# Two interleaved attention and MLP layers on one core: five of ten stretches of the instruction order rearranged

## The chip, the cores and the metric

The kernel runs on one core of a Trainium2 chip. The metric is the device time of one execution in microseconds (us). Before the change the median of three runs is 442.16 us (441.85 to 442.31).

The engines in the text are PE (TensorE, matrix products), DVE (VectorE), ACT (ScalarE), POOL (GpSimd) and SP (SyncE, which issues the DMAs). PEld is PE's weight load, which runs beside its products. Each engine works through a queue of its own in order; semaphores make one engine wait for another.

## The reference

An attention layer A and an MLP layer B act on x of 2048 rows and 512 columns, and the pair is applied twice, with the same weights, in bf16. Cut to what matters:

```python
qkv = (x @ wqkv) ...                     # 32 heads of 16 columns
scores = einsum("bhqd,bhkd->bhqk", q, k) * Dh ** -0.5
mask = (i - j >= 0) & (i - j < 256)      # sliding window of 256 rows
p = softmax(where(mask, scores, -1e9))
A = einsum("bhqk,bhkd->bhqd", p, v) ... @ wo

B = gelu(x @ w1 + b1) @ w2 + b2          # w1: 512 x 1792, w2: 1792 x 512

x = x + A(layernorm(x)); x = x + B(layernorm(x))   # and both lines once more
```

## The kernel before

**Tiles and stages.** The 2048 rows are 16 tiles of 128 rows; with two passes there are 32 tiles. Attention works on blocks of 256 rows, 16 in all, numbered on through both passes (block b of the text is the b-th). The MLP works on ten jobs of two or four tiles (`JOBS`).

For one block of attention the steps are, with the lines of the program: layer norm (`bn_stats` and `bn_aggr` on DVE, L599 and L601; two small steps on POOL for the reciprocal root, L611 and L617; `xn` on DVE, L627), a transposing DMA on SP (L632) into `xnTA`, projections to q, k and v on PE (L653) with evacuations from PSUM (q and v: a cast on DVE L588 or ACT L590; k: L687 on DVE, which multiplies by a parity mask and writes `KT`), scores on PE (L754, a "score group" of four PSUM banks), Exp on ACT (L761, two for each group, into `E`), a multiplication of parts of `E` by `mask01` (L782, on DVE or on POOL), the P·V products on PE (L804; two for each block), a transpose of their result on DVE (L813, `OD`), reciprocal and normalisation (L817, L821), a second transpose (L827), the output projection on PE (L653 again, from `OT` and `Wo_sb`) and the residual addition on DVE (L849). For a job of the MLP: layer norm and transposing DMA into `xnTB`, products with `W1_sb` on PE (L653), for six of the 14 row chunks a bias addition on DVE (L871) and Gelu on ACT (L874), for the others Gelu with bias on ACT (L879), products with `W2_sb` (L653), and the residual addition (L887 on POOL, L894 on DVE). The bf16 values of a V tile are copied once more, shifted by half a tile, with DMAs (L702).

**What sets the order.** The whole program is first recorded as a list of 3098 nodes, each an operation with what it reads and writes (`_Plan.add`). It is then issued in the order of a table of node numbers, `_ORDER`. A second table, `_ALT`, names the nodes that run on their alternative engine (masks and normalisations: POOL for DVE; casts: ACT for DVE). A third, `_BANKS`, gives the PSUM bank for each allocation in the order in which the allocations come. The program is thus interleaved by hand-made tables, not by a planner at build time:

```python
for i in _ALT:
    nodes[i]["eng"], nodes[i]["fn"] = nodes[i]["alts"][1]
banks = iter(_BANKS)
...
for i in _ORDER:
    nd = nodes[i]
    assert nd["deps"] <= seen
    ...
    for g, k in nd["alloc"]:
        b = next(banks)
        gmap[g] = tuple(range(b, b + k))
```

`_Sched.op` then goes through the nodes in this order and puts each into the queue of its engine, with semaphore waits for what it reads, for the buffers that it overwrites and for the earlier users of its PSUM banks. So a bank number can make one instruction wait for another that has nothing to do with its data. Attention of a block, projections for the next two blocks and pieces of MLP jobs stand mixed on PE's queue, and the same on the others.

## Time and profile before

| | before |
|---|---|
| median of the runs (lowest, highest) | 442.16 us (441.85, 442.31) |
| span of the profiled execution | 442.4 us |
| PE busy | 416.1 us (94%) |
| ACT busy | 386.4 us (87%) |
| DVE busy | 341.0 us (77%) |
| POOL busy | 212.7 us (48%) |
| instructions | 16864 |

The profile is one execution; its span is the time from its first to its last instruction, and it stands 0.24 us above the median of the runs. A row of a timeline gives the start, the length, the engine, the line, the operation, the tiles that it writes and reads and, in brackets, the idle time ahead of it with what ended that. A row of the groups gives, after the count, busy time and the mean length of one in ns, then the idle time ahead of the group. The first slices of the span are the load of x and the weights; the last are the second pass's MLP alone.

### The profile page before, as it was taken

Reading aid. Unit: us, or ns where it says so; the run is one execution under the profiler, and the core shown is the slowest. Engines: PE = TensorE matmul, PEld = TensorE weight load, DVE = VectorE, ACT = ScalarE, POOL = GpSimd, SP = SyncE. Lnnn points to the kernel's source line nnn. Section 1 sums busy time; section 2 is a strip of 40 time slices with the busy share of each in tenths; the row PEclk is TensorE's granted clock in tenths of the full one; section 3 lists DMA queues with packets and bytes.
Section 4 is the critical chain, followed back from the end, with each engine's and each line's share of the span. In section 5 each row is a group of like instructions: output and inputs, shape, how many; then the busy total and the mean of one; then the engine's idle time right before and its main releaser. Section 6 shows DMA issues by size and latency. Waiting matters only on the chain.

```text
span 442.4 us, 16864 instructions
## 1 busy us (share of the span) xinstructions
PE 416.1 (94%) x7523; PEld 233.2 (53%) x7593; DVE 341.0 (77%) x638; ACT 386.4 (87%) x458; POOL 212.7 (48%) x236
## 2 busy tenths in 40 slices
PE   8997999988789997999999999999999999999997
PEld 4555657544444563554455455455555464444675
DVE  7997789788785599967698868877888576746762
ACT  4997999999889999889899989999897988999533
POOL 3566344363442674711575454634728165804411
PEclk9999999999899999999999999999999999999999
DMA  7686422004101012121031021100421014003002
GB/s 234 184 209 185 87 64 45 20 10 69 39 3 25 16 34 56 28 46 24 4 65 31 1 57 26 34 20 10 69 39 20 20 39 105 14 1 81 15 0 73
DMA packets 48116, 23.25 MB, mean 53 GB/s; under 512 B 33196, under 2 KB 48044, under 8 KB 48044
## 3 DMA queue, kind: packets, MB, share of 16 engines
q1 hardware_dynamic: 48044, 22.17, 22.2%
q8 instruction: 60, 0.98, 0.9%
q14 instruction: 12, 0.10, 0.1%
HBM read 8.00 MB, written 2.10 MB: 23 GB/s over the span
## 4 chain that ended last, share of the span: by engine, by line
PE 79%; ACT 11%; DVE 6%; issue 2%; DMA 1%; DVEq 0%
PE ps L653 59%; PE ps L754 9%; PE ps L804 9%; ACT E L761 9%; DVE OD L813 1%; PE ps L539 1%; DVE stat L599 1%; DVE X L849 1%; DMA xnTB<-xn 1%; ACT gT L879 1%; ACT L879 1%; DVE KT L687 1%; DVE E L782 0%; PE ps L639 0%; ACT QT L590 0%
## 5 line engine op out<-in xcount | busy, mean ns | idle before, releaser
L761 ACT ACTIVATE E<-ps 128x1024 bf16<-128x1024 f32 x300 | 284.2, 1033 | 28.7 <-PE ps L754 28.0
L782 POOL TENSOR_TENSOR E<-E,mask 128x512 bf16<-128x512 bf16 (+2 forms) x111 | 120.9, 1106 | 91.3 <-ACT E L761 91.0
L653 PE MATMUL ps<-W_sb,gT 128*128 128x512 bf16 (+1 forms) x434 | 112.2, 373 | 3.2 <-issue 2.2
L653 PE MATMUL ps<-xnTB,W_sb 128*128 128x512 bf16 (+1 forms) x541 | 107.8, 336 | 3.4 <-issue 1.8
L653 PEld LDWEIGHTS ps<-xnTB,W_sb 128*128 128x128 bf16 x560 | 52.0, 98 | 42.9 <-issue 4.1
L653 PE MATMUL ps<-xnTA,Wqkv_sb 128*128 128x256 bf16 x512 | 70.7, 273 | 0.9 <-ACT E L761 0.4
L782 DVE TENSOR_TENSOR E<-E,mask 128x512 bf16<-128x512 bf16 (+2 forms) x125 | 60.1, 500 | 13.3 <-ACT E L761 12.9
L754 PE MATMUL ps<-QT,KT 32*128 32x128 bf16 (+3 forms) x1920 | 60.3, 231 | 9.8 <-ACT E L761 5.6
L653 PEld LDWEIGHTS ps<-W_sb,gT 128*128 128x128 bf16 x462 | 41.2, 98 | 41.1 <-issue 3.6
L754 PEld LDWEIGHTS ps<-QT,KT 32*128 32x128 bf16 x1920 | 28.5, 92 | 59.1 <-ACT E L761 34.9
L653 PEld LDWEIGHTS ps<-xnTA,Wqkv_sb 128*128 128x128 bf16 x512 | 47.4, 98 | 20.2 <-issue 2.9
L813 DVE STREAM_TRANSPOSE OD<-ps 128x1024 f32<-128x1024 f32 x32 | 39.9, 1246 | 21.3 <-PE ps L804 20.7
L887 POOL TENSOR_TENSOR Xb<-X,b2all 128x512 f32<-128x512 bf16 x32 | 37.7, 1180 | 34.3 <-DVE X L894 33.9
L879 ACT ACTIVATE gT<-ps,b1T 128x512 bf16<-128x512 f32 (+1 forms) x80 | 42.6, 609 | 9.5 <-PE ps L653 9.4
L804 PE MATMUL ps<-E,Va 64*17 64x128 bf16 (+3 forms) x1920 | 44.3, 234 | 1.9 <-issue 0.8
L821 POOL TENSOR_TENSOR Nb<-OD,Rc 128x512 bf16<-128x512 f32 x25 | 26.4, 1058 | 38.7 <-DVE Rc L817 29.8
L804 PE MATMUL ps<-E,Vs 64*17 64x128 bf16 (+3 forms) x1920 | 44.9, 234 | 0.0
L599 DVE BATCH_NORM_STATS2 stat<-X 128x6 f32<-128x512 bf16 x64 | 42.9, 679 | 0.5
L804 PEld LDWEIGHTS ps<-E,Va 64*17 64x17 bf16 x1920 | 37.2, 85 | 11.6 <-issue 9.0
L871 DVE TENSOR_SCALAR gT<-ps,b1T 128x512 bf16<-128x512 f32 (+1 forms) x60 | 36.8, 632 | 6.6 <-PE ps L653 6.2
L687 DVE TENSOR_TENSOR KT<-ps,parmask 128x1024 bf16<-128x1024 f32 x32 | 38.7, 1211 | 3.6 <-PE ps L653 3.6
L804 PEld LDWEIGHTS ps<-E,Vs 64*17 64x17 bf16 x1920 | 38.0, 85 | 0.2
(55 smaller groups left out, 348.8 us busy)
## 6 DMA issues: line engine op xcount, KB each, us to landing
Vs<-Va SPq DMA_DIRECT2D x64, 68.0 KB, 2.0
W_sb<-in_B_w_dram SPq DMA_DIRECT2D x4, 512.0 KB, 4.8
out_dram<-X SPq DMA_DIRECT2D x15, 128.0 KB, 1.8
X<-in_A_x_dram SPq DMA_DIRECT2D x3, 512.0 KB
Wqkv_sb<-in_A_wqkv_dram SPq DMA_DIRECT2D x4, 256.0 KB, 4.5
W_sb<-in_B_w_dram SPq DMA_DIRECT2D x2, 384.0 KB, 7.1
W_sb<-in_B_w_dram SPq DMA_DIRECT2D x1, 768.0 KB, 5.0
Wqkv_sb<-in_A_wqkv_dram SPq DMA_DIRECT2D x1, 512.0 KB, 6.7
```

The costliest lines, as they stand in the source:

```text
L599: add("dve", lambda e, B, t=t, k6=k6: e.bn_stats(stat6[:, k6, :], X[:, t, :]), reads=["X%d" % t], writes=["st%d" % k6], key="bs%d" % (k + j))
L653: r = e.matmul(ps[:, B[g][0], cols], lhsT, rhs, start=st, stop=sp)
L687: add("dve", lambda e, B, g=g, i=i: e.tensor_tensor(out=KT[:, kb, 2 * i : 2 * i + 2].rearrange("p c m a q -> p a (c m) q"), in0=ps[:, B[g] ...
L754: x = e.matmul(ps[:, bk[r], o : o + n], KT[rows, kb, c, m].rearrange("p a q -> p (a q)"), QT[rows, c, q : q + n], start=True, stop=True)
L761: add("act", lambda e, B, g_=g_, gi=gi: e.activation(E[:, 2 * gi : 2 * gi + 2, e0 : e0 + 512], ps[:, B[g_][0] : B[g_][0] + 2, :], AF.Exp, ...
L782: fn = lambda e, B: e.tensor_tensor(out=Ew, in0=Ew, in1=Mw, op=ALU.mult)
L804: x = e.matmul(ps[32 * r : 32 * r + VW, B[g][par], c % 2 * 2 * P + lo : c % 2 * 2 * P + hi], V[rows, (2 * b + m // 2) % VR, c * HC + 2 * r ...
L813: add("dve", lambda e, B: e.transpose(OD[:, s].rearrange("p a c q -> p (a c q)"), ps[:, B[g][0] : B[g][0] + 2, :]), reads=["ps:" + g], wri ...
L821: return e.tensor_tensor(out=Nb[:, s, :].rearrange("p (k a d) -> p a k d", a=2, d=Dh), in0=sums[:, :, :, 0:Dh], in1=rc[:, :, :, None].to_b ...
L871: add("dve", lambda e, B, g=g, fc=fc: e.tensor_scalar(out=gT[:, fc, c0 : c0 + M], in0=ps[:, B[g][0], 0:M], scalar1=b1T[:, fc : fc + 1], sc ...
L879: add("act", lambda e, B, g=g, fc=fc: e.activation(gT[:, fc, c0 : c0 + M], ps[:, B[g][0], 0:M], AF.Gelu_apprx_tanh, bias=b1T[:, fc : fc + ...
L887: add("pool", lambda e, B, t=t, xs=xs: e.tensor_tensor(out=Xb[:, xs, :], in0=X[:, t, :], in1=b2all[:], op=ALU.add), reads=["X%d" % t, "b2a ...
```

## The change

The three tables get other numbers. The program's order has nine places that no operation crosses, and with them ten stretches. In five of these the nodes stand in another order; in the other five the queue of each engine is as it was. The stretches that change lie, by the times of the profile before, at 0 to 31.2 us, 31.2 to 67.5, 110.7 to 160.7, 160.7 to 198.0 and 290.2 to 341.4; they are called the first, second, fourth, fifth and eighth in the text. `_ALT` has 162 entries in place of 172: DVE has 16 operations more, POOL 15 less and ACT one less. The 15 from POOL are ten masks (L782), two normalisations (L821) and three of the small layer-norm additions (L611); casts change between DVE and ACT in both directions, one net to DVE. 139 of 658 bank numbers differ. Nothing else of the program changes; its lines after the tables stand 7 lower in number (L842 is what L849 was).

```diff
 _ORDER = [
-    15, 34, 5, 0, 6, 14, 35, 7, 33, 28, 38, 29, 47, 8, 18, 23, 9, 36, 3, 26, 31, 10, 57, 37, 11, 22, 1, 40, 4, 24,
...
+    34, 0, 15, 5, 8, 35, 3, 14, 6, 16, 38, 23, 47, 33, 19, 4, 29, 9, 36, 7, 57, 1, 21, 10, 37, 11, 28, 58, 40, 12, 61,
...
 _ALT = [
...
 _BANKS = [
```

The first place is DVE's queue in the second stretch, where block 3 is projected and block 1 is attended to; before the change it runs at 33 to 40 us. `KT` is the evacuation of a K projection, `E` a mask, `xn` the layer norm's result, `OD` the transpose behind a P·V product. Before:

```order
L782 TENSOR_TENSOR E<-E,mask01 128x4x128
L782 TENSOR_TENSOR E<-E,mask01 128x4x192
L849 TENSOR_TENSOR X<-X,ps 128x512 x2
L599 BN_STATS stat6<-X 128x6 x2
L601 BN_AGGR statmv<-stat6 128x2 x2
L687 TENSOR_TENSOR KT<-ps,parmask 128x2x8x64
L627 TENSOR_SCALAR xn<-X,statmv,rstd 128x512 x2
L813 STREAM_TRANSPOSE OD<-ps 128x1024
L687 TENSOR_TENSOR KT<-ps,parmask 128x2x8x64
```

And now:

```order
L775 TENSOR_TENSOR E<-E,mask01 128x4x128
L842 TENSOR_TENSOR X<-X,ps 128x512
L775 TENSOR_TENSOR E<-E,mask01 128x4x64
L592 BN_STATS stat6<-X 128x6
L775 TENSOR_TENSOR E<-E,mask01 128x4x192 x2
L842 TENSOR_TENSOR X<-X,ps 128x512
L680 TENSOR_TENSOR KT<-ps,parmask 128x2x8x64
L592 BN_STATS stat6<-X 128x6
L594 BN_AGGR statmv<-stat6 128x2 x2
L806 STREAM_TRANSPOSE OD<-ps 128x1024
L620 TENSOR_SCALAR xn<-X,statmv,rstd 128x512 x3
L680 TENSOR_TENSOR KT<-ps,parmask 128x2x8x64
```

A mask of 64 columns for each of four parts (256 in all) and one of 192 (768) have come in ahead of the second `KT`, the two `xn` of this block's MLP input stand behind the `OD` transpose, and a third `xn` stands with them.

The second place is PE's queue at the same time, from the end of block 1's first P·V product. Scores have `QT,KT`, projections `xnTA`, the MLP `xnTB`. Before:

```order
L653 MATMUL ps<-xnTA,Wqkv_sb 128x256 x12
L754 MATMUL ps<-QT,KT 128x256 x8
L653 MATMUL ps<-xnTA,Wqkv_sb 128x256 x6
L754 MATMUL ps<-QT,KT 128x192 x8
L754 MATMUL ps<-QT,KT 128x128 x4
L653 MATMUL ps<-Wqkv_sb,xnTA 128x512 x8
L754 MATMUL ps<-QT,KT 128x192 x8
L754 MATMUL ps<-QT,KT 128x128 x4
L653 MATMUL ps<-xnTB,W1_sb 128x256 x8
```

And now:

```order
L747 MATMUL ps<-QT,KT 128x256 x8
L646 MATMUL ps<-xnTA,Wqkv_sb 128x256 x12
L747 MATMUL ps<-QT,KT 128x192 x8
L747 MATMUL ps<-QT,KT 128x128 x4
L646 MATMUL ps<-xnTA,Wqkv_sb 128x256 x4
L646 MATMUL ps<-Wqkv_sb,xnTA 128x512
L747 MATMUL ps<-QT,KT 128x192 x8
L747 MATMUL ps<-QT,KT 128x128 x4
L646 MATMUL ps<-Wqkv_sb,xnTA 128x512 x7
L747 MATMUL ps<-QT,KT 128x128 x8
L747 MATMUL ps<-QT,KT 128x64 x16
L646 MATMUL ps<-xnTB,W1_sb 128x256 x16
```

The first score group has moved ahead of twelve projection products, the second ahead of a few, and the last score group (128x128 and 128x64) ahead of the MLP's first pieces. The first V projection (`Wqkv_sb,xnTA`) now stands ahead of a score group, and its bank is the one that the second `KT` evacuation frees.

The third place is DVE's queue in the fourth stretch, behind block 4's first P·V product, with the bias additions (`gT`) of the third MLP job; before the change it runs at 119 to 126 us. Before:

```order
L813 STREAM_TRANSPOSE OD<-ps 128x1024
L871 TENSOR_SCALAR gT<-ps,b1T 128x512
L599 BN_STATS stat6<-X 128x6
L871 TENSOR_SCALAR gT<-ps,b1T 128x512
L782 TENSOR_TENSOR E<-E,mask01 128x4x128
L817 RECIPROCAL Rc<-OD 128x32
L871 TENSOR_SCALAR gT<-ps,b1T 128x512 x2
L782 TENSOR_TENSOR E<-E,mask01 128x4x192
L871 TENSOR_SCALAR gT<-ps,b1T 128x512
L782 TENSOR_TENSOR E<-E,mask01 128x4x192
```

And now:

```order
L806 STREAM_TRANSPOSE OD<-ps 128x1024
L810 RECIPROCAL Rc<-OD 128x32
L775 TENSOR_TENSOR E<-E,mask01 128x4x128
L864 TENSOR_SCALAR gT<-ps,b1T 128x512
L775 TENSOR_TENSOR E<-E,mask01 128x4x128
L864 TENSOR_SCALAR gT<-ps,b1T 128x512
L775 TENSOR_TENSOR E<-E,mask01 128x4x128
L775 TENSOR_TENSOR E<-E,mask01 128x4x64
L864 TENSOR_SCALAR gT<-ps,b1T 128x512
L775 TENSOR_TENSOR E<-E,mask01 128x4x64
L864 TENSOR_SCALAR gT<-ps,b1T 128x512
L775 TENSOR_TENSOR E<-E,mask01 128x4x192
```

More masks stand between the bias additions; they come from POOL's queue and from earlier or later places on DVE's.

## The prediction

> **What bounds the kernel now.** I read the page's busy line first, then the windows of each reordered stretch, and last the timelines of all engines in the places where TensorE (PE) stands still.

> ```profile
> PE 416.1 (94%) x7523; PEld 233.2 (53%) x7593; DVE 341.0 (77%) x638; ACT 386.4 (87%) x458; POOL 212.7 (48%) x236
> ```

> PE is the bound on average. The windows below are cut at the ends of the stretches (the third is left as it is); after the start, their columns are length, then busy time of PE, PEld, DVE, ACT and POOL, PE's granted clock, DMA share and GB/s.

> ```profile
> 0.00:31.20 31.20, 28.14 (x409) 17.21 (x413) 28.06 (x57) 25.22 (x33) 15.77 (x31) 1.00 0.78 205
> 31.20:67.50 36.30, 33.52 (x576) 21.02 (x579) 30.07 (x62) 32.85 (x43) 17.75 (x19) 1.00 0.47 119
> 67.50:110.70 43.20, 39.36 (x908) 24.29 (x905) 36.33 (x68) 41.32 (x52) 21.02 (x22) 1.00 0.20 35
> 110.70:160.70 50.00, 45.63 (x912) 24.49 (x923) 35.19 (x71) 45.40 (x51) 24.20 (x25) 0.97 0.13 25
> 160.70:198.00 37.30, 33.49 (x713) 18.59 (x717) 32.84 (x63) 33.38 (x37) 20.37 (x24) 1.00 0.21 39
> 290.20:341.40 51.20, 50.08 (x954) 27.73 (x962) 41.55 (x72) 45.55 (x52) 25.52 (x28) 1.00 0.19 30
> ```

> PE lacks 3.06, 2.78, 3.84, 4.37, 3.81 and 1.12 us in them. No order can give back more than its own stretch lacks, so the five that change hold 15.1 us at the very most, and the last of them 1.1. A loss has no such ceiling. In the untouched stretch from 67.5 us ACT works 41.32 of 43.20 us; in the others nothing is saturated, and the gaps are waits of one engine for another. The largest in the second stretch lie here, on PE:

> ```profile
> 37.90 0.40 PE L754 MATMUL ps<-QT,KT 32*128 32x256 bf16 x8
> 38.23 0.83 PE L653 MATMUL ps<-xnTA,Wqkv_sb 128*128 128x256 bf16 x6
> 40.28 0.40 PE L754 MATMUL ps<-QT,KT 32*128 32x192 bf16 x12 [1.23 <-ACT E L761]
> 40.85 1.67 PE L653 MATMUL ps<-Wqkv_sb,xnTA 128*128 128x512 bf16 x7 [0.16 <-issue]
> 43.58 1.03 PE L653 MATMUL ps<-xnTB,W_sb 128*128 128x256 bf16 x8 [0.73 <-DMA xnTB<-xn]
> 44.55 0.41 PE L754 MATMUL ps<-QT,KT 32*128 32x128 bf16 x24
> ```

> Two real gaps: 1.23 us for an Exp to free score banks, 0.73 us for the transposing DMA that brings the MLP's input: 1.96 us together. DVE (first four rows), ACT (two) and the DMA queue (the last) at the same time:

> ```profile
> 35.94 1.19 DVE L687 TENSOR_TENSOR KT<-ps,parmask 128x1024 bf16<-128x1024 f32 x1
> 37.23 0.74 DVE L627 TENSOR_SCALAR xn<-X,statmv,rstd 128x512 bf16<-128x512 bf16 x2
> 37.88 1.25 DVE L813 STREAM_TRANSPOSE OD<-ps 128x1024 f32<-128x1024 f32 x1
> 39.04 1.19 DVE L687 TENSOR_TENSOR KT<-ps,parmask 128x1024 bf16<-128x1024 f32 x1
> ...
> 36.91 0.60 ACT L590 ACTIVATE QT<-ps 128x512 bf16<-128x512 f32 x1 [0.67 <-PE ps L653]
> 38.35 1.94 ACT L761 ACTIVATE E<-ps 128x1024 bf16<-128x1024 f32 x2 [0.84 <-PE ps L754]
> ...
> 37.71 2.96 SPq L632 DMA_TRANSPOSE xnTB<-xn  x2
> ```

> DVE runs from 35.94 to 40.23 without a pause, and ACT twice waits for PE. This is where the second stretch is decided.

> **The change part by part.** The computation, the tiles and the buffers stay; what changes is the place of instructions in the queues, 16 more instructions on DVE, and PSUM bank numbers. The durations for what is moved:

> ```profile
> L599 DVE BATCH_NORM_STATS2 stat<-X 128x6 f32<-128x512 bf16 x64 | 42.9, 679 | 0.5
> ...
> L782 DVE TENSOR_TENSOR E<-E,mask 128x512 bf16<-128x512 bf16 x59 | 29.6, 513 | 4.7 <-ACT E L761 4.6
> L627 DVE TENSOR_SCALAR xn<-X,statmv,rstd 128x512 bf16<-128x512 bf16 x64 | 26.6, 431 | 3.2 <-POOL rstd L617 1.6 <-issue 1.2 <-DVE E L782 0.3
> L782 DVE TENSOR_TENSOR E<-E,mask 128x768 bf16<-128x768 bf16 x47 | 26.0, 571 | 8.3 <-ACT E L761 8.2
> L782 DVE TENSOR_TENSOR E<-E,mask 128x256 bf16<-128x256 bf16 x19 | 5.4, 285 | 0.3 <-ACT E L761 0.2
> ...
> L821 POOL TENSOR_TENSOR Nb<-OD,Rc 128x512 bf16<-128x512 f32 x25 | 26.4, 1058 | 38.7 <-DVE Rc L817 29.8 <-DVE statmv L601 8.9
> ...
> L782 DVE TENSOR_TENSOR E<-E,mask x125: 229/426/1401, 20.2 to 412.4; 128x512 bf16<-128x512 bf16 x59, 128x768 bf16<-128x768 bf16 x47, 128x256 bf16<-128x256 bf16 x19
> ...
> DMA to landing us min/median/max: 2.4/2.5/4.1
> ```

> *First stretch (to 31.2 us): 0.0.* The queues begin alike but for a few independent steps. On POOL a normalisation of 1.06 us (L821) now stands ahead of a mask that a P·V product waits for. The product comes later by part of that, I take 0.4; ACT's 0.67 and 0.84 us of idle time behind it take that up. Without that cover it would be +0.4 to +1.1.

> *Second stretch (31.2 to 67.5): +1.1.* On DVE one mask of 256, one of 768 and one xn more now stand ahead of block 3's second KT evacuation: 0.285 + 0.571 + 0.431 = 1.29 us. It ended at 40.23; it would end at 41.5, or 41.2 to 41.9 with the masks' own waits for Exp. The bank that it frees is now the one that the first V projection needs, and that began at 40.85. From it to the MLP's first piece PE has 1.67 (V, 7 of whose 8 matmuls the trace has) + 0.40 + 0.41 us of work (the two score groups; the second now comes ahead of the MLP pieces): 2.48 us. So PE is there at 44.0 (43.7 to 44.4). Before it was through the same work and 1.03 us of MLP pieces at 44.96. With 1.03 added for these the new order stands at 45.0, level, if the MLP input is there. It is not: its two xn now wait behind the OD transpose and two masks, and the second ends at about 40.4 (40.0 to 40.8) in place of 37.96. The DMA lands 2.4 to 4.1 us after its issue and two of them occupy the queue for 2.96; I count landing at 44.6 (43.3 to 45.9). Then PE stands at 44.6 + 1.03 = 45.6 against 44.96: +0.7. One mask more on DVE, 0.285 to 0.571, lies ahead of the mask that this block's second P·V product waits for: +0.4. From 44 to 67 us PE has hardly a gap to make it up, and the stretch behind it keeps its order, so I carry the sum on. Ends: −0.6, if the KT evacuation comes before 41.0 and the DMA hides (of 1.96 us of gap the wait for KT, some 1.4, alone is left); +1.9, if the transfer lands at 45.9 (46.9 − 44.96).

> *Fourth stretch (110.7 to 160.7): −0.3.* Here a slow clock counts.

> ```profile
> 113.10:116.50 3.40, 1.69 (x32) 1.02 (x28) 3.05 (x7) 3.40 (x5) 0.23 (x1) 1.00 0.20 41
> 116.50:119.90 3.40, 2.89 (x138) 2.16 (x132) 0.71 (x1) 3.00 (x4) 1.22 (x2) 0.50 0.20 41
> 38.00:41.40 3.40, 2.02 (x29) 1.22 (x27) 2.48 (x3) 3.05 (x4) 1.03 (x1) 1.00 0.40 77
> ...
> 119.19 1.25 DVE L813 STREAM_TRANSPOSE OD<-ps 128x1024 f32<-128x1024 f32 x1 [2.75 <-PE ps L804]
> 123.67 1.61 DVE L871 TENSOR_SCALAR gT<-ps,b1T 128x512 bf16<-128x512 f32 x2 [0.28 <-PE ps L653]
> ```

> For 3.4 us behind a window in which PE worked only 1.69 of 3.40 us its clock was 0.50: 2.89 us of work that takes 1.45 at full clock. The new order puts some pieces more of projections into that thin window. If the clock then stays up, the OD transpose comes up to 1.45 us earlier. Behind it DVE now has three masks of 512 and two of 256 (2.11 us) up to the fourth bias add, where one mask of 512 and a bn_stats of 0.679 stood (1.19 us): 0.9 us longer, less the 0.28 that it waited. So −1.45 + 0.9 − 0.28 = −0.8. If the clock falls all the same, the longer DVE row is left, partly hidden because ACT sets the next score group: +0.2 (at most +0.6). I take the middle, −0.3. The rest of the stretch keeps ACT's amount of work, 45.40 of 50.00, and I cost it at nothing; uncovered, a mask of 0.5 us would show.

> *Fifth stretch (160.7 to 198): +0.1.* Three steps move ahead of what they waited behind (an OD transpose ahead of a residual add, a mask ahead of a V cast, a V projection behind a score group), each worth up to 0.5; one score group's banks now wait for the OD transpose and a P·V product for masks that went to DVE, each up to 0.5. −0.5 to +0.5.

> *Eighth stretch (290.2 to 341.4): +0.3.*

> ```profile
> 319.02 1.03 PE L653 MATMUL ps<-Wo_sb,OT 128*128 128x512 bf16 x4 [0.16 <-issue]
> ...
> 318.91 1.94 ACT L761 ACTIVATE E<-ps 128x1024 bf16<-128x1024 f32 x2 [0.53 <-PE ps L754]
> 320.95 0.60 ACT L590 ACTIVATE Va<-ps 128x512 bf16<-128x512 f32 x1
> ```

> The score group ahead of ACT's 0.53 us wait now stands behind three more output-projection pieces, 3 × 1.03/4 = 0.77: ACT waits about 1.3. A V cast of 0.60 leaves ACT behind it and gives most of that back: +0.2. Another piece waits for a residual of the MLP, 0.3 at most; I take 0.1 of it. PE lacks only 1.12 us here, so there is little to gain: −0.3 to +0.7.

> Sum: 0.0 + 1.1 − 0.3 + 0.1 + 0.3 = **+1.2**. The profiled execution's span is 442.4, 0.24 above the median of 442.16 (442.4 lies just above the slowest of the three runs); 442.4 + 1.2 − 0.24 = 443.4. About 0.2%, 0.88 us, is what a measurement of this kernel can tell from no change.

> **The rivals.** *R1, slower: the late KT evacuation trips the clock.* The window 38.0:41.4 had 2.02 us of work and kept the clock; 1.69 lost it at 116.5. If the wait for KT takes it towards 1.7, the next 3.4 us run at half: 3.4 × 0.5 = +1.7. Then 445.1. For it: the gap grows in one place and the score group moves out ahead of it. Against: two pieces of q projection come into it. [...]

> *R2, faster: the clock stays up at 116.5 and the second stretch ends at its low end.* −0.6 − 0.8, the others at 0: −1.4, so 440.8. It decides if block 3's second KT evacuation ends before 41.0. For it: the two score groups that ACT waits for (0.67, 0.84) come earlier in PE's queue. Against: the 1.29 us more on DVE.

> *R3, it cancels:* second stretch +0.9, fourth −0.9, 442.2. Or the orders do what they say and other waits end last anyway.

> *R4, slower: DVE's masks wait behind POOL.* Masks on DVE took 229 to 1401 ns, median 426: some waited 0.97 us in themselves. Ten more masks lie on DVE; if six of them, at places that PE waits for, take the longest, 6 × 0.97 = 5.8, less 0.8 from the fourth stretch: +5.0, 447.2. It decides if the moved masks' mean goes past 1 us. Against: a median of 426 says that this is rare. [...]

> **How the numbers follow.** Forecast 0.40 at 443.4; R1 0.14; R2 0.25; R3 0.15; R4 0.06. Faster is R2, 0.25; same is R3, 0.15; slower the rest, 0.60. The range reaches from R2 with 0.4 us of its own doubt below (440.4) to R1 with 0.9 above (446.0), and leaves out R4 and tails. The forecast's own range is 443.0 to 444.6.

> **What would show it.** Right: the first V projection of block 3 begins 0.4 to 1.1 us after 40.85, behind L680 on DVE; the first piece from xnTB waits for its DMA longer than 0.73; at 67.5 us of before the new trace is 0.6 to 1.5 late; the granted clock near 116.5 is up, or fallen and the fourth stretch a little longer; from 198 us on the distance stays but for the eighth stretch. Wrong: a new trace that stands level or early at 67.5; a half clock in a place that had none; a mean of the moved masks above 1 us; a stretch left as it is that changes its length by over 1 us, since I carry lags through those unchanged.

## The result, and the profile after

The changed kernel takes 447.88 us (446.32 to 449.35), the kernel before 442.24 us beside it: ratio 1.0124, 95% interval 1.0095 to 1.0152. The forecast was 443.4 with a range up to 446.0. The direction was right, the size was not, and the largest part of the loss lies in a stretch that the change leaves alone.

Of the page of the changed kernel, the busy line; of its windows, the six that answer to those of before (cut where its own stretches end; the columns are the same):

```profile
PE 425.6 (95%) x7593; PEld 231.5 (52%) x7593; DVE 346.2 (78%) x654; ACT 386.2 (87%) x457; POOL 198.4 (44%) x221
```

```profile
0.00:31.00 31.00, 28.27 (x411) 16.66 (x411) 28.02 (x58) 25.09 (x32) 15.53 (x29) 1.00 0.80 207
31.00:67.30 36.30, 34.36 (x581) 21.30 (x580) 30.60 (x62) 32.79 (x43) 15.04 (x18) 1.00 0.48 116
67.30:113.85 46.55, 40.69 (x913) 24.32 (x905) 36.95 (x71) 41.13 (x51) 20.93 (x22) 1.00 0.19 35
113.85:163.30 49.45, 46.21 (x924) 23.75 (x927) 37.92 (x75) 45.80 (x52) 19.15 (x22) 1.00 0.12 25
163.30:200.65 37.35, 33.92 (x715) 18.02 (x708) 32.99 (x65) 32.85 (x36) 19.21 (x21) 1.00 0.22 39
293.10:345.35 52.25, 51.84 (x963) 27.60 (x962) 42.73 (x76) 45.49 (x52) 22.27 (x23) 1.00 0.14 30
```

The third row is the surprise: 46.55 us against 43.20, for the same instructions in the same order. Where the time goes is seen on PE inside block 2's first P·V product (timeline of the changed kernel):

```profile
69.21 0.24 PE L797 MATMUL ps<-E,Va 64*17 64x128 bf16 x4
69.25 0.23 PE L797 MATMUL ps<-E,Vs 64*17 64x128 bf16 x2
72.39 0.22 PE L797 MATMUL ps<-E,Vs 64*17 64x128 bf16 x2 [2.92 <-issue]
```

One node of the program, one product after the other from the same tiles; the first has waited for all that the node needs. And yet PE stands for 2.92 us between two of them, and the trace names no releaser, only "issue". What happens in this time is seen in the DMA queues: first, of the changed kernel, those of 65 to 69.9 us and then those of 69.9 to 71 us, and below, of the kernel before, those of 65.2 to 68 us. The columns are packets, MB and the time of the packets as a share of 16 engines.

```profile
q1 hardware_dynamic: 1168, 0.33, 33.0%
...
q8 instruction: 1, 0.02, 5.3%
```

```profile
q1 hardware_dynamic: 624, 0.20, 33.9%
q8 instruction: 1, 0.02, 2.1%
```

Queue q8, which the profile calls "instruction", is taken for the one that carries PE's instructions, one packet of 16 KB at a time, by its count: it has 60 packets in the whole trace (0.98 MB), and PE's 15350 instructions are just under 60 times 256. In the kernel before the packet for this place starts at 66.10 us, three microseconds ahead of the instruction that needs it (at 69.10). In the changed kernel it starts at 69.96, 0.5 us behind the end of PE's last product (69.48), and PE goes on 2.43 us later.

The profile of before has a trap of its own. In the runs, the time is the span plus 1.7 to 1.9 us (448.17 against 446.4 in the profiled one). So the profiled execution of before, with its span of 442.4, was one of about 444.2, not one near the median. It holds the half-clock window at 116.5 us (3.4 us at 0.50), and few runs have one anywhere: of the 50 runs of that kernel beside the experiments six show a mean clock of 0.996, all others 0.999 or 1.0. The stretches are therefore compared with a profile without such a window, that of experiment e4 (the kernel before but for six products at its start; median 442.55 us, span of the profile 441.2):

| stretch | e4, us | changed | difference | forecast |
|---|---|---|---|---|
| first | 31.00 | 30.92 | −0.08 | 0.0 |
| second | 36.31 | 36.28 | −0.03 | +1.1 |
| third (same order) | 43.24 | 46.56 | +3.32 | 0 |
| fourth | 49.12 | 49.44 | +0.32 | −0.3 |
| fifth | 36.78 | 37.35 | +0.57 | +0.1 |
| sixth, seventh (same order) | 92.29 | 92.44 | +0.15 | 0 |
| eighth | 51.18 | 52.27 | +1.09 | +0.3 |
| ninth, tenth (same order) | 98.22 | 98.09 | −0.13 | 0 |

A stretch ends here with its last PE product. The sum is +5.2 us, which is the difference of the two spans. Each column is one execution.

### The profile page after: what moved, and what is told of

Its sections match the earlier page's. It is cut to its first block, busy times and chain, and to the rows that moved or that the text cites. A ratio compares the mean times of both kernels' runs of the same rounds, so it can differ in the third digit from the quotient of the medians.

```text
span 446.4 us, 16928 instructions
## 1 busy us (share of the span) xinstructions
PE 425.6 (95%) x7593; PEld 231.5 (52%) x7593; DVE 346.2 (78%) x654; ACT 386.2 (87%) x457; POOL 198.4 (44%) x221
## 4 chain that ended last, share of the span: by engine, by line
PE 80%; DVE 12%; ACT 5%; issue 2%; POOL 0%; DVEq 0%
PE ps L646 62%; PE ps L747 9%; PE ps L797 9%; ACT E L754 5%; DVE OD L806 2%; DVE stat L592 2%; DVE E L775 1%; DVE gT L864 1%; DVE KT L680 1%; DVE xn L620 1%; DVE X L842 1%; DVE OT L820 1%; DVE Va L581 0%; DVE X L887 0%; DVE Nb L814 0%
## 5 line engine op out<-in xcount | busy, mean ns | idle before, releaser
L754 ACT ACTIVATE E<-ps 128x1024 bf16<-128x1024 f32 x300 | 284.1, 1034 | 32.2 <-PE ps L747 31.1
L775 POOL TENSOR_TENSOR E<-E,mask 128x512 bf16<-128x512 bf16 (+2 forms) x101 | 108.5, 1089 | 70.7 <-ACT E L754 70.7
L646 PE MATMUL ps<-W_sb,gT 128*128 128x512 bf16 (+1 forms) x462 | 117.8, 374 | 0.2 <-DVE OD L806 0.2
L646 PE MATMUL ps<-xnTB,W_sb 128*128 128x512 bf16 (+1 forms) x560 | 112.6, 337 | 1.3 <-issue 1.1
L646 PEld LDWEIGHTS ps<-xnTB,W_sb 128*128 128x128 bf16 x560 | 51.8, 98 | 42.9 <-issue 3.4
L646 PE MATMUL ps<-xnTA,Wqkv_sb 128*128 128x256 bf16 x512 | 71.6, 273 | 0.7 <-ACT xnTA L583 0.3
L775 DVE TENSOR_TENSOR E<-E,mask 128x768 bf16<-128x768 bf16 (+2 forms) x135 | 63.8, 496 | 9.6 <-ACT E L754 9.4
L646 PEld LDWEIGHTS ps<-W_sb,gT 128*128 128x128 bf16 x462 | 41.4, 98 | 41.1 <-issue 3.0
L646 PEld LDWEIGHTS ps<-xnTA,Wqkv_sb 128*128 128x128 bf16 x512 | 46.9, 98 | 21.9 <-issue 3.1
L880 POOL TENSOR_TENSOR Xb<-X,b2all 128x512 f32<-128x512 bf16 x32 | 37.3, 1171 | 41.6 <-DVE X L887 41.2
L814 POOL TENSOR_TENSOR Nb<-OD,Rc 128x512 bf16<-128x512 f32 x23 | 24.6, 1068 | 58.2 <-DVE Rc L810 58.2
L797 PE MATMUL ps<-E,Vs 64*17 64x128 bf16 (+3 forms) x1920 | 44.3, 230 | 2.9 <-issue 2.9
L797 PE MATMUL ps<-E,Va 64*17 64x128 bf16 (+3 forms) x1920 | 43.6, 230 | 2.6 <-issue 1.1
L797 PEld LDWEIGHTS ps<-E,Va 64*17 64x17 bf16 x1920 | 36.8, 84 | 12.5 <-issue 8.7
L592 DVE BATCH_NORM_STATS2 stat<-X 128x6 f32<-128x512 bf16 x64 | 42.9, 678 | 0.4
L680 DVE TENSOR_TENSOR KT<-ps,parmask 128x1024 bf16<-128x1024 f32 x32 | 38.7, 1211 | 2.4 <-PE ps L646 1.7
L797 PEld LDWEIGHTS ps<-E,Vs 64*17 64x17 bf16 x1920 | 37.6, 84 | 3.2 <-issue 3.1
```

Of the source, the lines that this page charges most:

```text
L592: add("dve", lambda e, B, t=t, k6=k6: e.bn_stats(stat6[:, k6, :], X[:, t, :]), reads=["X%d" % t], writes=["st%d" % k6], key="bs%d" % (k + j))
L646: r = e.matmul(ps[:, B[g][0], cols], lhsT, rhs, start=st, stop=sp)
L680: add("dve", lambda e, B, g=g, i=i: e.tensor_tensor(out=KT[:, kb, 2 * i : 2 * i + 2].rearrange("p c m a q -> p a (c m) q"), in0=ps[:, B[g] ...
L754: add("act", lambda e, B, g_=g_, gi=gi: e.activation(E[:, 2 * gi : 2 * gi + 2, e0 : e0 + 512], ps[:, B[g_][0] : B[g_][0] + 2, :], AF.Exp, ...
L775: fn = lambda e, B: e.tensor_tensor(out=Ew, in0=Ew, in1=Mw, op=ALU.mult)
L797: x = e.matmul(ps[32 * r : 32 * r + VW, B[g][par], c % 2 * 2 * P + lo : c % 2 * 2 * P + hi], V[rows, (2 * b + m // 2) % VR, c * HC + 2 * r ...
```

## The experiments

These theories are named in the expectations. F: PE's instructions come in blocks of 256, and a late block stops PE. Q: the queues of the reordered stretches cost what they cost, as the prediction had it. D, L: a transposing DMA, or the load of a weight, is what makes the block late. S, N: the transposes, or the load, have no part in that.

### Which stretch: e1 and e2

e1 puts the second stretch's pieces of the three tables back to before; e2 takes them alone from the changed kernel. (Here and below `_ORDER` lists the unchanged stretches as the kernel before does; each engine's queue in them is the same in both kernels.)

```diff
 e1 = changed kernel
-_ORDER[248:518], its entries of _ALT and _BANKS: as changed
+_ORDER[248:518], its entries of _ALT and _BANKS: as before
 e2 = kernel before
-_ORDER[248:518], its entries of _ALT and _BANKS: as before
+_ORDER[248:518], its entries of _ALT and _BANKS: as changed
```

> The changed kernel with the second stretch put back to its order before; the other four stretches stay rearranged. Theory F (instruction fetch): PE's instructions come in blocks of 256, a block that is late stops PE inside a P.V product, and the second stretch's order delays one such block by 4 us through its transposing DMAs at 66 to 69 us. Then the 3 us lost behind 69 us go: about 444.5 to 445. Theory Q (the prediction's): the second stretch costs through its own queues, 1.1 us: about 446.8, and PE's stop inside the P.V product stays.

> The kernel before with the second stretch alone rearranged. Theory F: PE stops for about 3 us inside block 2's first P.V product, in a stretch that is not rearranged: about 445. Theory Q: the second stretch itself gets 1.1 us longer: 443.3, no stop.

e1: 445.17 us, 1.0073 of before (1.0054 to 1.0092), near F and far from Q; the third stretch is back at 43.24. e2: 446.22 us, 1.0086 (1.0070 to 1.0101), above both. So the second stretch's order brings more than half of the loss, +3.6 alone, and the other four bring +2.6. The profile of e2 is its fastest run (445.37) and shows a part of that: the second stretch itself is 1.84 longer than in e4, the third 0.67. In the second stretch two things add up: what the prediction described, the V projection that waits for block 3's second KT evacuation (first row), and a stop without a releaser, of which the next part treats (second row). F's stop of 3 us did not come here; the third stretch has one of 0.36.

```profile
42.42 0.39 PE L646 MATMUL ps<-Wqkv_sb,xnTA 128*128 128x512 bf16 x1 [1.90 <-DVE KT L680]
...
55.94 0.72 PE L646 MATMUL ps<-xnTB,W_sb 128*128 128x256 bf16 x5 [0.59 <-issue]
```

The same place in the changed kernel:

```profile
39.55 0.32 PE L747 MATMUL ps<-QT,KT 32*128 32x192 bf16 x8 [0.38 <-issue]
40.98 0.39 PE L646 MATMUL ps<-Wqkv_sb,xnTA 128*128 128x512 bf16 x1 [0.57 <-DVE KT L680]
43.33 0.41 PE L747 MATMUL ps<-QT,KT 32*128 32x128 bf16 x24
43.97 1.25 PE L646 MATMUL ps<-xnTB,W_sb 128*128 128x256 bf16 x10 [0.23 <-issue]
```

Behind the old first stretch the V projection comes at 42.42, 0.9 later than the 41.5 that the prediction took; behind the new one at 40.98. So the second stretch's price depends on the order of the first. And the wait for the MLP's input (0.73 us before) is down to 0.23 in the changed kernel: the last score group stands ahead of it.

### What a stop is: e3 to e6

Where do stops without a releaser lie? Counting PE's instructions from the start (two for each weight load and its product, one for each wait that stands by itself), worked out from the traces of several kernels:

```text
kernel             stop begins  instructions  count + 63  weight loads  packet's start
                   at, us       before it                 pause, us     to restart, us
changed               69.25        2241        9 x 256       3.14          2.43
e2                    54.97        1729        7 x 256       0.97          2.25
e2                    71.41        2241        9 x 256       0.36          2.27
e3 (12 fewer)         70.03        2241        9 x 256       0.95          2.81
before                39.49        1218        5 x 256 + 1   0.80          2.46
e5 (16 more)          38.14        1217        5 x 256       2.07          2.65
e5                   107.62        3777       15 x 256       1.90          2.67
e6 (48 more)          37.34        1218        5 x 256 + 1   3.16          2.45
e6                   185.03        6593       26 x 256       2.08          2.60
```

These lie where the count is 63 short of a multiple of 256, or one past it, and PE goes on 2.2 to 2.8 us behind the start of the packet. So do, to within two instructions, all ten gaps of PE over 1.1 us that the 14 traces put down to "issue". Shorter ones also lie elsewhere: 0.58 us at 94 to 100 us in every kernel, 0.91 us at 178.70 in the changed one. Numbered in order, the k-th packet starts about when PE comes to the k-th boundary, and the stop stands at the next one: the packet of 69.96 us is the 8th, the stop is at 9 x 256. In the traces of the kernel before and of the changed one PE's first weight load behind boundary k + 1 comes 2.34 us or more behind the start of packet k, at all 59 boundaries in each. So between one boundary and the next PE has the time of 256 instructions, while the packet took about 1 us to its start (the median is 0.95 and 0.96 us in the two) and, at the stops of the table, 2.25 to 2.81 us more. A whole P·V product (L804 before, L797 now) is 128 weight loads and 128 products and takes 1.4 us (68.11 to 69.55 us in the kernel before): a block that falls into it is used up in less than those 2.25 us. Most crossings show no stop: of the changed kernel's 60, the weight loads pause by 0.6 us or more behind a fetch at two, for 0.63 and 3.14 us.

The direct test shifts the boundaries and keeps every other queue as it is. At the start PE runs warm-up products whose result nobody uses. e3 and e4 leave out six short ones (32 columns each), e5 and e6 add 8 and 24 short ones.

```diff
 e3 (changed kernel), e4 (kernel before)
         for i in order:
             nd = PL.nodes[i]
+            if nd["key"] in ("warm2", "warm9", "warm10", "warm11", "warm14", "warm16"):
+                continue
 e5, e6 (kernel before), x = 8 and 24 for warm17, else 0
-            e.matmul(ps[:, B[g][0], 0:n], ...)
+            [e.matmul(ps[:, B[g][0], 0:n], ...) for _ in range(1 + x)][-1]
```

> The changed kernel without six of the short and long warm-up products at its start, which no result uses: PE's instruction stream is 12 shorter, everything else is the same. Theory F: all block boundaries move 12 instructions on in the program; by the positions of the boundaries and a fetch of 3.4 us behind each crossing, the stops of PE sum to 0.0 to 1.3 us in place of 3.2 to 5.7: 443.5 to 445, a remainder of the stop near 69 us possible. Theory Q: no change, 447.9 within 0.5.

> The kernel before without the same six warm-up products (PE's stream 12 instructions shorter). Theory F: stops of 2.6 to 5.3 us sink to 0.0 to 0.7: 437.5 to 440. Theory Q: no change, 442.2 within 0.5.

> The kernel before with eight more short warm-up products (32 columns) at its start: PE's instruction stream is 16 longer from there on, nothing else moves. Theory F (PE's instructions come in blocks of 256, and a block that comes late stops PE): the stops seen so far all lie where the count of PE's instructions is 63 short of a multiple of 256, give or take one. With the count shifted by 16, boundaries fall where PE goes through a whole block faster than the next can come: +4.6 us by a fetch that starts 0.9 us behind the crossing and 2.43 us more to the restart, up to +8 with slow fetches: 447 to 450, with new stops in stretches whose order is the same. Theory Q (the queues of the reordered stretches alone matter): the start gets at most 0.8 us later, 442.6 to 443.4.

> The same with 24 more short warm-up products (PE's stream 48 longer). Theory F: stops of 12 to 16 us in all (at about 37, 52, 107, 121, 182, 197, 242, 319 and 424 us by the positions of the boundaries): 454 to 459. Theory Q: the start up to 2.4 us later, 442.6 to 445.

e5: 448.60 us, 1.0136 (1.0101 to 1.0171). e6: 457.70 us, 1.0341 (1.0300 to 1.0382). Both within what F gave, far from Q: 8 and 24 products of 32 columns, which delay the end of the first stretch by 0.2 and 0.6 us, cost 6.1 and 15.2 us in all. The order is that of the kernel before throughout, and the stops are new or longer. Added up, the weight loads' pauses of over 0.33 us behind a fetch are about 1.7 us in the kernel before, 8.0 in e5 and 13.5 in e6, and of the nine places that F named for e6 seven show one. Four of e6's stops are followed by a half-clock window of 3.4 us (at 40.66, 125.99, 187.43 and 248.87 us); the changed kernel's stop of 3.1 us, in its profile, is not: PE works 0.48 us from 69.00 to 72.40, and the clock is 1.00 from 72.40 to 75.80. One of e6's stops on PE, inside a P·V product, and its mean clock:

```profile
185.02 0.26 PE L797 MATMUL ps<-E,Vs 64*17 64x192 bf16 x3
187.11 0.25 PE L797 MATMUL ps<-E,Vs 64*17 64x192 bf16 x1 [1.83 <-issue]
```

```profile
core 0: 458.3 us, clock 0.985
```

And e5's first stop on PE, at 38.5 us, which tears the products of one score group apart:

```profile
38.12 0.39 PE L747 MATMUL ps<-QT,KT 32*128 32x256 bf16 x7
40.21 0.28 PE L747 MATMUL ps<-QT,KT 32*128 32x256 bf16 x1 [1.69 <-issue]
```

The other direction failed as a forecast. e4: 442.55 us, 1.0004 (0.9993 to 1.0015), no gain, where F promised 2 to 5 us; e3: 446.96 us, 1.0098 (1.0074 to 1.0121), 0.9 us below the changed kernel and within its spread, where F promised 443.5 to 445. F had taken the kernel before to hold 2.6 to 5.3 us of stops. Its trace shows pauses of 0.80, 0.58 and 0.37 us behind a fetch, e4's 0.68 and 0.56: there was little to gain. In e3 the stop at 69 us shrinks to 0.95 and lies 12 instructions further in the program, at the same count.

### What makes the block late: e7 to e11

The stop at 69.25 needs more than an unlucky boundary, since the boundary is the same before the change. PE comes to the one that asks for the block at 65.2 to 65.3 us in both (the start of the last weight load before it); the packet starts 0.9 us later before, 4.6 us later in the changed kernel. In the new order transposing DMAs of two late xn are issued at 65.18 and 67.10 us (before: 64.23 and 66.15), and the load of the last piece of W2, issued at 47.8 us in place of 31.6, runs at 49 to 52 us, when another block is asked for.

```diff
 e7 (changed kernel): xn34, xn35 (nodes 439, 441) ahead of ke4_1 (549)
-    ... 549, ..., 439, ..., 441, ...
+    ... 439, 441, 549, ...
 e8 (kernel before): xn34 behind ke4_1, xn35 behind two masks more (581, 586), their DMAs behind them
-    ... 439, ..., 441, ..., 549, ..., 581, ..., 586, ...
+    ... 549, ..., 439, 581, ..., 586, 441, ...
 e9 (changed kernel): load ldz3 (54) ahead of tx32 (243);  e10: e7 and e9 together
-    ... 243, ..., 54, 359, ...
+    ... 54, 243, ..., 359, ...
 e11 (kernel before): ldz3 (54) ahead of vs6_1 (359)
-    ... 54, ..., 243, ..., 359, ...
+    ... 243, ..., 54, 359, ...
```

> The changed kernel with two operations of DVE moved back: the layer norm's results for block 1's MLP input (two xn) go ahead of block 4's second KT evacuation again, in place of behind it and behind a cast and a mask. Their transposing DMAs then leave at 64 to 65 us in place of 65.2 and 67.1, before PE crosses a block boundary at 64.8. Theory D (the fetch was late because it waited for these transposes): the fetch starts within 2 us of the crossing and the stop of 3 us near 69 us shrinks to under 0.5: about 445.2. Theory S (the lateness has nothing to do with the transposes): the stop stays between 0.4 and 3.1 us: 446.5 to 448.

> The kernel before with the same two xn moved late, behind block 4's second KT evacuation and two masks, and their transposes with them. No product needs them within 5 us. Theory D: the transposes meet the instruction fetch at 66 to 69 us and PE stops for 1 to 3 us inside block 2's first P.V product: 443.6 to 445.6. Theory S: 442.6 within 0.5.

> The changed kernel with one DMA of SP moved back: the load of the last piece of W2 (384 KB), which the new order issues at 47.8 us, goes ahead of block 0's MLP transposes again (as in the kernel before, which issues it at 31.6 us). Theory L (the load's packets, 49 to 52 us, delay the instruction fetch for which PE crosses a boundary at 49.7, and the following ones with it): the fetch behind 49.7 us starts 0.4 to 1.0 us after its crossing in place of 1.5 to 3.0, and the stops at 54 to 55 and at 69 us get rarer: 445.5 to 446.5, 1.5 to 2.5 below the changed kernel. Theory N (the load has no part in it): 447.9 within 0.7.

> The changed kernel with the load and the two xn moved back together. If late DMAs of either kind are what delays the fetches: no stop over 0.4 us at the boundaries at 54 and 69 us in the profile, and the time that the other four stretches leave: 444.8 to 445.5. If the lateness has another cause: 446.5 to 448.

> The kernel before with that load alone moved late, to the place that it has in the new order. Theory L: a fetch 1.5 to 3 us late behind 49.7 us, a stop of up to 1 us at 54 us, and at times one at 69: 443.3 to 445. Theory N: 442.5 within 0.4.

| | time, us | ratio to before (95%) |
|---|---|---|
| e7 | 446.61 | 1.0091 (1.0061 to 1.0120) |
| e8 | 442.69 | 0.9999 (0.9986 to 1.0012) |
| e9 | 449.23 | 1.0149 (1.0115 to 1.0183) |
| e10 | 448.43 | 1.0124 (1.0098 to 1.0149) |
| e11 | 442.66 | 0.9992 (0.9979 to 1.0005) |

Neither D nor L is borne out: e7 lies where S put it, e8 and e11 show no loss, e9 and e10 lie even above what N and "another cause" gave. So late transposes or a late load cost nothing in the kernel before, and moving them back in the changed kernel leaves its loss (e9, e10). e8 is the weaker test of D: in its profile the first late transpose leaves at 68.29 us, behind the packet's start at 67.47, so the two did not meet. In e7's profile, its fastest run, the stop at 69 us is gone and a shorter one stands at 54.8, but its runs reach from 445.26 to 448.10 us. e10 says most: the load is early, the transposes leave at 63.57 and 65.50 us (the second still 0.4 us behind PE's coming to the boundary), the queue is idle from 67.5 us on, and the stop is there all the same. Its queues at 65.1 to 69.1 us, then at 69.1 to 70.3 us:

```profile
q1 hardware_dynamic: 905, 0.26, 32.2%
...
q8 instruction: 1, 0.02, 5.3%
```

The stop that is left in e7, and the one of e9, on PE:

```profile
54.83 0.72 PE L646 MATMUL ps<-xnTB,W_sb 128*128 128x256 bf16 x5 [0.52 <-issue]
```

```profile
72.35 0.23 PE L797 MATMUL ps<-E,Vs 64*17 64x128 bf16 x2 [2.63 <-issue]
```

In e10 PE comes to the boundary at 65.13 us and the packet starts at 69.17, 4.0 us later, though the DMA engines moved nothing from 67.5 on. So it stays open why this block's fetch starts late in the new order. What the traces suggest is that lateness goes with the program and not with chance alone: the packet of the 42nd boundary (at about 300 us; in the changed kernel no other transfer runs from 299 to 304) starts 2.8 to 3.0 us behind PE's coming to it in all six profiles that have the eighth stretch reordered and the boundaries in the same place, and −0.5 to 0.2 us in five with the old order. It may go with the place of the boundary too: with 12 instructions fewer (e3) the packet asked for at 67 us starts 1.1 us later in place of 4.6, in one profile of each.

### The eighth stretch alone: e12

```diff
 e12 = kernel before
-_ORDER[2048:2407], its entries of _ALT and _BANKS: as before
+_ORDER[2048:2407], its entries of _ALT and _BANKS: as changed
```

> The kernel before with the eighth stretch alone rearranged. By the changed kernel's profile, where that stretch is 1.1 us longer without one gap of PE over 0.4 us: 443.5 to 443.9, a number of waits of 0.1 to 0.4 us in it and no stop at a block boundary. The prediction's own term: +0.3, 442.8.

443.55 us, 1.0019 (1.0006 to 1.0032). Its window for the stretch, and two of PE's waits:

```profile
288.40:340.70 52.30, 51.05 (x955) 27.63 (x962) 42.71 (x76) 45.52 (x52) 22.29 (x23) 1.00 0.14 30
```

```profile
313.56 1.05 PE L646 MATMUL ps<-xnTA,Wqkv_sb 128*128 128x256 bf16 x8 [0.16 <-DVE KT L680]
315.09 0.60 PE L646 MATMUL ps<-Wo_sb,OT 128*128 128x512 bf16 x2 [0.15 <-DVE X L887]
```

The stretch is 1.1 us longer than in e4's profile, the kernel 0.9 in the median, as expected and not as the prediction's +0.3. PE has no gap over 0.2 us there, and no stop at a boundary. The two waits shown, for a KT evacuation and for a residual, make 0.3 us; the rest is spread over delays that the trace does not add up, and which of them cost it is not shown.

## Why the prediction was wrong, step by step

**What bounds the kernel.** PE, as said. But the working took every stop of PE for a wait of one engine for another, and "issue" for records that are missing. The 1.23 us ahead of the score group at 40.28, which the trace puts down to ACT and which is the heart of the second stretch's working, ends 2.46 us behind the start of an instruction packet, at 1218 instructions: about two thirds of it (0.80 us by the weight loads) were such a stop. In e4, where the boundary lies 12 instructions (six products) further on, the same group starts at 39.45, and the stop tears it apart behind six products:

```profile
39.45 0.34 PE L747 MATMUL ps<-QT,KT 32*128 32x192 bf16 x6 [0.46 <-ACT E L754]
40.14 0.31 PE L747 MATMUL ps<-QT,KT 32*128 32x192 bf16 x6 [0.35 <-issue]
```

And what PE "lacks" in a window of the profile before is in part missing records: that trace has 7523 of 7593 products. e4's trace has them all, and there PE is busy throughout the eighth stretch:

```profile
288.85:340.00 51.15, 51.13 (x963) 27.67 (x962) 41.41 (x72) 45.42 (x52) 25.37 (x28) 1.00 0.21 30
```

**The span and the median.** The profiled execution was taken to stand 0.24 us above the median; by the runs' own spans it stands about 2 us above. The fourth stretch's gain of 0.8 was priced from a half-clock window that most runs do not have. In the changed kernel's profile it is gone, and the profile of before is 0.7 longer there; against a profile without it the stretch loses 0.3.

**First stretch.** 0.0 forecast, −0.08: right in size; the waits behind it were not followed.

**Second stretch.** +1.1 forecast. The wait for KT is there but short (0.57 us; the V projection at 40.98, where the working had 41.5), the wait for the MLP's input, taken to grow, shrinks to 0.23, and the stretch comes out level at −0.03. Taken alone (e2) it costs 1.84, but some 0.6 to 1.0 of that is a stop at a boundary, which the working did not know. That the forecast said "slower" was luck in good part: its largest term did not come.

**Third stretch: the step that failed.** The prediction says of the second stretch's lag: "the stretch behind it keeps its order, so I carry the sum on." It set the third stretch's own change at nothing. That stretch keeps its order and loses 3.3 us. In its place the runs showed a stop of PE of 3.1 us at 69.25 us, for a block of 256 instructions whose packet starts 4.6 us behind the crossing in place of 0.9. Of the whole difference of 5.6 us this is the largest part, and no rival had it. The prediction named as signs of error "a stretch left as it is that changes its length by over 1 us" and a trace "that stands level or early at 67.5", and both came: the second stretch ends at 67.20 us, against 67.31 before.

**Fifth and eighth.** +0.57 for +0.1, just outside the −0.5 to +0.5; +1.09 for +0.3, outside its 0.7. PE's two largest gaps in the fifth are one ahead of a score group and one ahead of the MLP's pieces, neither at a boundary; how they make up the 0.57 was not followed further:

```profile
177.39 0.40 PE L747 MATMUL ps<-QT,KT 32*128 32x256 bf16 x8 [0.88 <-DVE statmv L594]
178.70 1.89 PE L646 MATMUL ps<-xnTB,W_sb 128*128 128x512 bf16 x8 [0.91 <-issue]
```

**The rivals.** R1 wanted a half clock behind the wait for KT; the profile after has none (mean clock 1.00), and its time is 448.17 all the same. The other three runs show a mean of 0.996, the mean of the profile of before with its one window of 3.4 us; where theirs lies no trace shows. That little work ahead costs the clock was the author's estimate from 1.69 us of work in 3.40 ahead of 116.5; the changed kernel kept it behind 0.48 us in 3.40 (69.00 to 72.40). R2's conditions came true (the second KT evacuation ends at 40.92, before 41.0; the clock is up at 116.5), but its gain of 1.4 us did not. R3's cancelling gain in the fourth stretch did not come either. Against R4 stands the masks' own row in the changed kernel, which reads 229 to 1402 ns with a median of 425, as before; their mean is 0.50 us in both traces. The longest of now, 1402 ns at 288.52 us, runs beside two masks on POOL; that it waits for them is not shown:

```profile
L775 DVE TENSOR_TENSOR E<-E,mask x135: 229/425/1402, 20.4 to 416.4; 128x512 bf16<-128x512 bf16 x60, 128x768 bf16<-128x768 bf16 x51, 128x256 bf16<-128x256 bf16 x24
```

## What to carry to other kernels

Here PE was busy for 95% of the span with 7593 products, and its stops behind a late instruction packet were as long as 3.16 us (e6). In a kernel like it, find PE's long stops without a releaser, count the instructions up to them, and see whether they fall on one grid. If they do, read a change that reorders or adds a handful of PE instructions with that in mind: in e5 16 more at the start brought a stop of 1.90 us as far behind as 107.62 us, and the order of before, with nothing else changed, lost 6.1 us with them and 15.2 with 48. And set a profile's span beside the spans of the runs before its stalls are priced: a window that one execution in eight has (six of 50 here) is not there to be won.
